# Sparse attention and a squared-ReLU layer in one kernel: the last four blocks' second product as seven half-size products

## The chip, the cores and the metric

The kernel runs on one core of a Trainium2 chip. The metric is device time in microseconds (us) of one execution; the engines are named as in the profile: PE is TensorE (PEld its weight loads), DVE is VectorE, ACT is ScalarE, POOL is GpSimd, SP is SyncE.

## The reference

Two layers follow each other. Attention has 8 batches, 8 heads, 576 positions and 64 columns a head; four heads look back over a local window of 32 positions, four see every 32nd position. The result, as 4608 tokens of 512 columns, goes through two products with a squared ReLU between them.

```python
scores = scale * np.matmul(q, k.transpose(0, 1, 3, 2))
mask_local = (rel >= 0) & (rel < stride)                      # heads 0 to 3
mask_strided = (rel >= 0) & (pos[None, :] % stride == pos[:, None] % stride)   # heads 4 to 7
attn = softmax of the masked scores
x = np.matmul(attn, v), laid out as [4608 tokens, 512]
h = x @ w_in                    # 512 to 2048
r = np.maximum(h, 0.0)
g = s * (r * r) + b
out = g @ w_out                 # 2048 to 512
```

## The kernel before, in words

**Attention.** A batch is four pairs of heads (m = 0, 1 local, m = 2, 3 strided). `pair_steps` writes each pair as steps: transposes of q and k (or transposing DMAs in later batches), scores into a bank of PSUM, exp on ACT and mask on DVE (L529, L537), p times v into an "a" bank (L567), reciprocal and normalisation on DVE (L582, L593) into `x_nat`. x is then transposed into `xT`, [512 columns as 4 × 128, tokens]: by TensorE in early batches (`xtrans`, L615), by a transposing DMA on SP for local pairs from batch 2 (`x_dma`, L645), and for strided pairs from batch 4 by a write to DRAM and a transposing read (`x_out` L637, `x_in` L641). `xT` holds all 4608 tokens.

**The two products.** Tokens are cut into 9 blocks of 512 (T = 0 to 8). The first product (`ff1`, L673) makes for each of the 16 row tiles `ft` four matmuls of 512 columns into one of two "f1" banks; ACT takes the ReLU (`u`, L691), DVE the square (`gT`, L697). `gT` has two buffers, so block T's first product begins after the second product of block T − 2. The second product (`ff2`, L713) takes 128 tokens at a time: 16 matmuls of 512 columns, with a weight load of `gT` before each, into one of two "f2" banks; DVE evicts it with the scale s and the bias row `bcs` (L724), and SP stores it (L728). The factor s and the bias b are folded into this eviction. The last 128 tokens are done as two halves of 256 columns.

**The order.** `Plan` is a small planner that runs while the program is built. Each step has a cost in ns, needs and keys; work of DVE, ACT, GpSimd and the DMA queues is posted with its needs and goes to the engine that ends it first. `Plan.LAT` adds the time until a result is seen: 70 ns for an engine, 12 us for a transposing DMA ("D", "Y"), 7 us for a write to DRAM ("X"). The main loop at the end chooses the next step of TensorE: attention if it is behind its due time (`due`) or nothing else is ready; else the next step of the first product; else of the second. When the first product is more than 64 steps ahead, the second goes first. The hardware then runs each engine's instructions in this order, with waits on what they need.

**PSUM.** Eight banks: t (1), s (2), a (1), f1 (2), f2 (2); `group_of` gives attention its banks.

**Buffers.** In the pool `inp`, the tags qp and kp (paired copies of q and k, later the outputs of transposing DMAs of q) have two buffers each.

Of the kernel before, what the change touches and what calls it, by code (L numbers as in the profile page):

```python
# [9 lines left out]
FP16 = mybir.dt.float16  # L10
# [5 lines left out]
class Plan:  # L16
# [20 lines left out]

    def post(self, needs, cost, fn, keys):
        self.pend.append((needs, cost, fn, keys))

    def flush(self):
        while True:
            best = None
            for p in self.pend:
                r = self.ready_at(p[0])
                if r is not None and r <= self.t and (best is None or r < best[0]):
                    best = (r, p)
            if best is None:
                return
            r, p = best  # L50
            self.pend.remove(p)
            eng = min(p[1], key=lambda e: max(self.free[e], r) + p[1][e])
            end = max(self.free[eng], r) + p[1][eng]
            self.free[eng] = end
            p[2](eng)
            for k in p[3]:
                if isinstance(k, Group):
                    k = ("rel", k.tag, k.n)
                soon = isinstance(k, tuple) and k[0] == "soon"
                self.done[k] = end + (6000.0 if soon else self.LAT[eng])  # L60

# [50 lines left out]
def kernel(  # L112
# [47 lines left out]
    gp = ctx.enter_context(tc.tile_pool(name="gp", bufs=2))  # L160
    op = ctx.enter_context(tc.tile_pool(name="op", bufs=3))
    psum = ctx.enter_context(tc.tile_pool(name="psum", bufs=1, space=bass.MemoryType.PSUM))

    ident = const.tile([128, 128], FP16)
    mask_loc = const.tile([128, LQ], FP16)
    mask_str = const.tile([SQ, SQ], FP16)
    neg_loc = const.tile([128, 2 * LQ], FP16)
    neg_str = const.tile([SQ, 2 * SQ], FP16)
    ones16 = const.tile([128, 128], FP16)
    s_sb = const.tile([128, 1], FP32)  # L170
# [4 lines left out]
    w_out_sb = const.tile([128, NFT, DM], FP16)  # L175
    bcs = const.tile([128, DM], FP32)
    NV = 2
    v_loc = [const.tile([128, 4, LT, D + 1], FP16, name=f"v_loc{i}") for i in range(NV)]
# [4 lines left out]
    qD_str = [const.tile([128, ST, 2, SQ], FP16, name=f"qD_str{i}") for i in range(2)]  # L183
    xT = [const.tile([128, NTOK], FP16, name=f"xT{i}") for i in range(4)]

# [117 lines left out]
    def pair_post(b, name, mm, key):  # L303

        if (b, name) not in paired:
            paired[b, name] = None

        def g(eng):
            if paired[b, name] is None:
                paired[b, name] = inp.tile([128, 2, LT, 2 * D], FP16, tag=name + "p",  # L310
                                           name=name + "p")[0:LQ]
            from_ = loaded[b, name + "l"]
            copy_on(eng, out=paired[b, name][:, mm].rearrange("p j (e d) -> p e j d", e=2),
                    in_=from_.rearrange("p (m e j d) -> p m e j d", m=2, e=2, d=D)[:, mm])
        plan.post([key], {"A": 810, "V": 350, **({"P": 900.0} if b in (1, 2, 3) else {})}, g,
                  [("in", name + "l", b, mm)])
# [34 lines left out]
    def group_of(kind, b, m, q=False):  # L351

        t, a, f1, f2 = ("t", TB), ("a", AB), ("f1", F1B), ("f2", F2B)
        banks = {"a": [a], "t": [t], "s": [("s", SB)]}[kind]
        if b == 0:
            banks = {"a": [f2, f2, f1], "t": [t, a], "s": [("s", SB), ("s", SB), f1]}[kind]
        elif b == 1 and kind == "a":
            banks = [f1, f1, a]
        elif b == 1 and q:
            banks = [t, f2]  # L360
        taken[kind] += 1
        return Group(*banks[taken[kind] % len(banks)])
# [4 lines left out]
    def pair_steps(b, m):  # L367
# [67 lines left out]
        q_by_dma = b >= (QB_DMA if loc else QS_DMA)  # L435
        x_by_dma = b >= (2 if loc else XS_DMA)

# [22 lines left out]
        def q_dma(eng):  # L460
            if loc:
                if (b, "qTl") not in loaded:
                    loaded[b, "qTl"] = inp.tile([128, 2, LT, LQ], FP16, tag="qp", name="qTl")
                st["qT"] = loaded[b, "qTl"][:, mm]
                nc.sync.dma_start_transpose(out=st["qT"],
                                            in_=loaded[b, "ql"][:, 768 * mm:768 * mm + 768])
                return
            if (b, "qT2") not in loaded:
                loaded[b, "qT2"] = inp.tile([128, 2, ST, SR], FP16,
                                            tag="vs" if b < KB_DMA else "kp", name="qT2")  # L470
            st["qT"] = loaded[b, "qT2"][:, mm]
            nc.sync.dma_start_transpose(out=st["qT"],
                                        in_=loaded[b, "qs"][:, 1024 * mm:1024 * mm + 1024])
# [137 lines left out]
        def xtrans(j, group):  # L611
# [10 lines left out]
            if j == nt - 1:  # L622
# [3 lines left out]
                def g(eng):  # L626
                    dst = xT[m][:, b * S:(b + 1) * S]
                    if loc:
                        copy_on(eng, out=dst, in_=st["px"])
                    else:  # L630
                        copy_on(eng, out=dst.rearrange("d (p j) -> d p j", j=nt),
                                in_=st["px"].rearrange("d (j p) -> d p j", j=nt))
                s.posts = [([key], {"A": 640, "V": 455 if loc else 756}, g, [("xT", b, m), group])]
            return s
# [5 lines left out]
        def x_in(eng):  # L640
            nc.sync.dma_start_transpose(out=xT[m][:, b * S:(b + 1) * S],  # L641
                                        in_=x_dram[2 * (b % 2) + mm])

        def x_dma(eng):
            nc.sync.dma_start_transpose(  # L645
                out=xT[m][:, b * S:(b + 1) * S].rearrange("d (t p) -> d t p", t=nt),
                in_=st["x"].rearrange("p t d -> p (t d)"))

        if x_by_dma and loc:
            plan.post([("x", id_, e, nt - 1) for e in range(2)], {"D": 1000.0}, x_dma,  # L650
                      [("xT", b, m)])
        elif x_by_dma:

            plan.post([("x", id_, e, j) for e in range(2) for j in (per - 1, nt - 1)],
                      {"X": 500.0}, x_out, [("xd", id_)])
            plan.post([("xd", id_)], {"Y": 1300.0}, x_in, [("xT", b, m)])
        else:
# [6 lines left out]
    gts = {}  # L664

    def ff1(T, ft, ct, group, cts=(0, 1, 2, 3), early=False):
        tok0 = T * PS
        def f():
            if ft == 0 and ct == cts[0]:
                gts[T] = gp.tile([128, NFT, PS], FP16, tag="gT", name="gT")  # L670
            if ct == cts[0]:
                gts["h", T, ft] = bank(group)
            nc.tensor.matmul(  # L673
                out=gts["h", T, ft], lhsT=w_in_sb[min(ft // 4, 2)][:, ct].rearrange(
                    "p (c x l) -> p c l x", x=128, l=4)[:, max(ft // 4 - 2, 0), ft % 4],
                rhs=xT[ct][:, tok0:tok0 + PS], start=(ct == cts[0]), stop=(ct == cts[-1]))

# [3 lines left out]
        if ft == 0 and ct == cts[0] and T >= 2:  # L681
            needs.append(("F2", T - 2))
        s = Step(f, 216, needs=needs, group=group if ct == cts[0] else None)
        if ct == cts[-1]:
            key = ("h", T, ft)
            s.keys = [key]

# [7 lines left out]
            def sq(eng):  # L695
                u = gts["u", T, ft]
                nc.vector.tensor_tensor(out=gts[T][:, ft, :], in0=u, in1=u, op=ALU.mult)  # L697

            free = [("g", *divmod(NFT * T + ft - 4, NFT))] if T or ft >= 4 else []
            s.posts = [([key] + free, {"A": 600, **({"V": 690} if T == 0 else {})}, rl, [("u", T, ft), group]),  # L700
                       ([("u", T, ft)], {"V": 430}, sq, [("g", T, ft)])]
        return s

    def ff2(T, ts, ft, group, part=0, parts=1):
# [14 lines left out]
        if ft == NFT - 1:  # L719
            s.keys = [id_] + ([("F2", T)] if ts == 3 else [])  # L720

            def ev(eng):
# [5 lines left out]
                nc.sync.dma_start(out=out[r0:r0 + 128, cols], in_=o[:, 0:n])  # L728
            s.posts = [([id_, ("bcs",)], {"V": 750 / parts + 60}, ev, [group])]
        return s  # L730
# [152 lines left out]
    for T in range(NBLK):  # L883
        if T == 0:
# [3 lines left out]
            f1 += [ff1(T, ft, ct, gr[ft], cts, True) for ct in cts for ft in range(4)]  # L888
        for ft in range(0 if T else 4, NFT):
            gr = Group("f2", F2B) if T == 0 and ft % 4 < 2 else Group("f1", F1B)  # L890
            for ct in range(4):
                f1.append(ff1(T, ft, ct, gr))
        if T == 0:

            gr = [Group(*x) for x in [("f2", F2B)] * 4 + [("a", AB)]]
            for c in range(0, NFT, 4):
                f2 += [bcs_step(ft, gr[4]) for ft in range(c, c + 4)]
                f2 += [ff2(T, ts, ft, gr[ts]) for ts in range(2) for ft in range(c, c + 4)]
            f2 += [ff2(T, ts, ft, gr[ts]) for ts in (2, 3) for ft in range(NFT)]
            continue  # L900
        for ts in range(4):

            parts = 2 if T == NBLK - 1 and ts == 3 else 1
            for part in range(parts):
                gr = Group("f2", F2B)
                for ft in range(NFT):
                    f2.append(ff2(T, ts, ft, gr, part, parts))
    def keep_running(until):

# [24 lines left out]
    def due():  # L934

        pos = (i1 + i2) / 64.0 + 0.1
        return (pos if pos <= 1 else 1 + (pos - 1) / 2) * batch_ns

    while i2 < len(f2) or any(at_i[p] < len(att[p]) for p in range(len(att))):
# [15 lines left out]
        if i2 < len(f2):  # L955
            order.append(2)
        if len(order) == 2 and i1 % 4 == 0 and i1 > i2 + 64:
            order.reverse()
# [55 lines left out]
```

## Time and profile before

| | us |
|---|---|
| median of 11 runs (lowest to highest) | 316.79 (315.63 to 318.9) |
| the profiled execution | 315.72 |
| its span, first to last instruction | 314.0 |
| TensorE busy in it | 307.7 |
| VectorE busy | 195.6 |
| ScalarE busy | 160.8 |
| GpSimd busy | 96.2 |

The span is what the trace of one execution covers; the profiled execution's own time is 1.7 us longer. Busy time of TensorE includes the modelled end of each matmul, which overlaps the next one: a mean of 379 ns stands for a matmul, though the next starts 216 ns after it. The distance between starts is what the text uses.

### The profile page before, as it was taken

Reading aid. Unit: us, or ns where it says so; the run is one execution under the profiler, and the core shown is the slowest. Engines: PE = TensorE matmul, PEld = TensorE weight load, DVE = VectorE, ACT = ScalarE, POOL = GpSimd, SP = SyncE. Lnnn points to the kernel's source line nnn. Section 1 sums busy time; section 2 is a strip of 40 time slices with the busy share of each in tenths; the row PEclk is TensorE's granted clock in tenths of the full one; section 3 lists DMA queues with packets and bytes.
Section 4 is the critical chain, followed back from the end, with each engine's and each line's share of the span. In section 5 each row is a group of like instructions: output and inputs, shape, how many; then the busy total and the mean of one; then the engine's idle time right before and its main releaser. Section 6 shows DMA issues by size and latency. Waiting matters only on the chain.

```text
span 314.0 us, 6164 instructions
## 1 busy us (share of the span) xinstructions
PE 307.7 (98%) x2268; PEld 171.2 (55%) x2268; DVE 195.6 (62%) x555; ACT 160.8 (51%) x304; POOL 96.2 (31%) x140
## 2 busy tenths in 40 slices
PE   8899999999999999999999999999999999999995
PEld 3765655666556565556555655555544454444444
DVE  6576868798967797658566867586732254333212
ACT  1876944788838688547037825661531263333100
POOL 7562559902960292058302850000000000000000
PEclk9999999999999999999999999999999999999999
DMA  7999999994999599979997999703041100110022
GB/s 126 201 212 204 215 165 151 221 158 110 79 155 171 85 127 143 147 137 141 163 179 178 123 168 147 185 35 106 21 90 43 57 35 0 67 37 33 34 100 70
DMA packets 99386, 37.84 MB, mean 121 GB/s; under 512 B 82394, under 2 KB 93274, under 8 KB 99354
## 3 DMA queue, kind: packets, MB, share of 16 engines
q0 software_dynamic: 57200, 18.08, 58.0%
q1 hardware_dynamic: 42154, 19.35, 30.5%
q8 instruction: 18, 0.29, 0.4%
q14 instruction: 14, 0.11, 0.1%
HBM read 36.84 MB, written 10.62 MB: 151 GB/s over the span
## 4 chain that ended last, share of the span: by engine, by line
PE 88%; DMA 8%; POOL 1%; issue 0%; SPq 0%; DVE 0%; POOLq 0%
PE ps_f L713 40%; PE ps_f L673 37%; PE ps_s L513 5%; DMA qs<-in_q_dram 4%; PE ps_a L567 4%; DMA w_out_sb<-in_v_dram 2%; DMA ql<-in_q_dram 2%; PE ps_t L395 1%; PE ps_a L736 1%; PE ps_t L615 1%; POOL v_loc L301 1%; PE ps_f L567 0%; SPq L807 0%; PE ps_f L395 0%; POOL ql L259 0%
## 5 line engine op out<-in xcount | busy, mean ns | idle before, releaser
L673 PE MATMUL ps_f<-xT,w_in_sb 128*128 128x512 f16 x568 | 145.5, 379 | 0.0
L713 PE MATMUL ps_f<-w_out_sb,gT 128*128 128x512 f16 (+1 forms) x592 | 144.7, 373 | 0.0
L691 ACT ACTIVATE u<-ps_f 128x512 f16<-128x512 f32 x140 | 82.7, 596 | 97.4 <-PE ps_f L673 84.3
L697 DVE TENSOR_TENSOR gT<-u 128x512 f16<-128x512 f16 x144 | 59.5, 417 | 46.7 <-ACT u L691 45.8
L673 PEld LDWEIGHTS <-w_in_sb 128*128 128x128 f16 x576 | 61.0, 113 | 44.5 <-issue 0.2
L713 PEld LDWEIGHTS <-gT 128*128 128x128 f16 x592 | 55.4, 98 | 52.4 <-DVE gT L697 0.6
L724 DVE SCALAR_TENSOR_TENSOR o<-ps_f,s_sb,bcs 128x512 f32<-128x512 f32 (+1 forms) x37 | 27.0, 729 | 24.9 <-PE ps_f L713 24.5
L593 DVE TENSOR_TENSOR x_nat<-ps_a,rec 72x256 f16<-72x256 f32 (+1 forms) x76 | 35.0, 460 | 1.3
L582 DVE RECIPROCAL rec<-ps_a 72x4 f32<-72x4 f32 (+1 forms) x76 | 13.8, 181 | 22.3 <-PE ps_a L567 21.8
L529 ACT ACTIVATE p_str<-ps_s 72x432 f16<-72x432 f32 (+1 forms) x46 | 20.9, 482 | 4.0 <-PE ps_s L513 3.7
L529 ACT ACTIVATE p_loc<-ps_s 128x384 f16<-128x384 f32 x46 | 21.0, 496 | 3.7 <-PE ps_s L513 3.1
L279 POOL DMA_DIRECT2D v_loc<-in_v_dram x28 | 20.8, 753 | 4.5 <-DMA kl<-in_k_dram 1.3
L567 PEld LDWEIGHTS <-p_str 72*128 72x128 f16 x256 | 15.4, 98 | 11.0 <-issue 0.2
L537 DVE TENSOR_TENSOR p_str<-p_str,mask_str 72x432 f16<-72x432 f16 (+1 forms) x42 | 14.6, 356 | 1.8 <-ACT p_str L529 1.3
L537 DVE TENSOR_TENSOR p_loc<-p_loc,mask_loc 128x384 f16<-128x384 f16 x42 | 14.0, 351 | 2.4 <-ACT p_loc L529 2.0
L768 POOL COPY gate<-kT 1x1 f16<-1x1 f16 x6 | 1.3, 215 | 45.2 <-DMA kT<-ks 45.2
L567 PE MATMUL ps_a<-v_str,p_str 72*128 72x65 f16 x204 | 14.9, 194 | 0.0
L567 PEld LDWEIGHTS <-p_loc 128*128 128x128 f16 x192 | 11.0, 98 | 6.7 <-ACT x_nat L588 0.3
L284 POOL DMA_DIRECT2D v_str<-in_v_dram x16 | 12.9, 814 | 5.1 <-DVE rec L582 2.8
L256 POOL DMA_DIRECT2D kl<-in_k_dram x16 | 11.8, 755 | 0.0
L923 PE MATMUL ps_f<-ones 128*128 128x512 f16 (+2 forms) x30 | 9.3, 446 | 1.4 <-DVE ones L230 1.1
L567 PE MATMUL ps_a<-v_loc,p_loc 128*128 128x65 f16 x150 | 10.5, 194 | 0.0
(116 smaller groups left out, 256.8 us busy)
## 6 DMA issues: line engine op xcount, KB each, us to landing
out_dram<-o SPq DMA_DIRECT2D x35, 256.0 KB, 4.4
w_out_sb<-in_moe_w_out_dram POOLq DMA_DIRECT2D x4, 512.0 KB, 11.1
v_loc<-in_v_dram POOLq DMA_DIRECT2D x28, 72.0 KB, 7.6
ql<-in_q_dram POOLq DMA_DIRECT2D x6, 288.0 KB, 7.0
qs<-in_q_dram POOLq DMA_DIRECT2D x6, 288.0 KB, 5.9
ks<-in_k_dram POOLq DMA_DIRECT2D x6, 288.0 KB, 7.2
kl<-in_k_dram POOLq DMA_DIRECT2D x4, 288.0 KB, 8.6
kl<-in_k_dram POOLq DMA_DIRECT2D x16, 72.0 KB, 4.2
```

The costliest lines, as they stand in the source:

```text
L279: nc.gpsimd.dma_start(out=vl[LPAD:128, h, :, 0:D], in_=v_band(b, h))
L513: nc.tensor.matmul(out=st["s", g][0:nk, c:c + 2 * nq], lhsT=(st["k"][:, i * nq:i * nq + nk] if loc else st["k"][:, i, 0:SQ]), rhs=st["q"][ ...
L529: nc.scalar.activation(out=pt[0:nk, 0:2 * n].rearrange("k t c -> k (t c)"), in_=st["s", g][0:nk, 0:2 * n * nq], func=AF.Exp, scale=scale)
L537: nc.vector.tensor_tensor(out=pt[0:nk, 0:2 * n], in0=pt[0:nk, 0:2 * n], in1=mask, op=ALU.mult)
L567: nc.tensor.matmul(out=st["a"][:, j % per, :], lhsT=st["pw", g][0:nk, i * nq:i * nq + WIDE], rhs=vt[0:nk, 2 * mm + e, j, :])
L582: nc.vector.reciprocal(out=st["rec", e, j][0:nq, 0:per], in_=st["pa", e, j][0:nq, 0:per, D:D + 1])
L593: nc.vector.tensor_tensor(out=st["x"][:, j0:j0 + per, 64 * e:64 * e + 64], in0=st["pa", e, j][0:nq, 0:per, 0:D], in1=st["rec", e, j][0:nq, ...
L673: nc.tensor.matmul(out=gts["h", T, ft], lhsT=w_in_sb[min(ft // 4, 2)][:, ct].rearrange("p (c x l) -> p c l x", x=128, l=4)[:, max(ft // 4 ...
L691: nc.scalar.activation(out=gts["u", T, ft], in_=gts["h", T, ft], func=AF.Relu)
L697: nc.vector.tensor_tensor(out=gts[T][:, ft, :], in0=u, in1=u, op=ALU.mult)
L713: nc.tensor.matmul(out=gts[id_], lhsT=gts[T][:, ft, ts * 128:(ts + 1) * 128], rhs=w_out_sb[:, ft, cols], start=(ft == 0), stop=(ft == NFT ...
L724: nc.vector.scalar_tensor_tensor(out=o[:, 0:n], in0=gts[id_], scalar=s_sb[:, 0:1], in1=bcs[:, cols], op0=ALU.mult, op1=ALU.add)
```

## The change

For blocks 5 to 8 (`SEVEN = 5`) the second product is computed in the form that makes a product of 2 × 2 blocks from seven block products (`ff2_seven`). The four blocks of the left side are halves of a block's 512 tokens by halves of the 2048 rows; those of the right side halves of those rows by halves of the 512 output columns. A product P1 to P7 is 2 × 8 matmuls of 256 columns. It needs:

- four differences of weights, once, after the second product of block 4 (`mix_post`): three into new tiles `w_mix`, one in place in `w_out_sb`; and the difference of the two halves of `bcs`;
- four sums of blocks of `gT` per block, each in two parts (`sums_post`), on DVE. In blocks 5 and 6 two of them overwrite `gT` itself once P1 and P2 have read it; in blocks 7 and 8 (`roomy`) they have tiles of their own;
- evictions that add what earlier evictions left: Va, Ua, Vb, and Ub = Ua + the difference of the bias on DVE or GpSimd; four stores of [128, 2, 256] per block (five in block 8). P2 continues the bank of P1 after Va is out, P4 that of P7 after Vb, P3 that of P5 after its store's eviction.

The order of products is P1 P2 P6 P7 P5 P4 P3 in blocks 5 and 6, all in the two f2 banks, and P1 P6 P7 P5 P2 P4 P3 in blocks 7 and 8, in four banks (f2 and s, then t, a and f1). The first product of blocks 5 to 8 takes its row tiles in the order 0-3, 8-11, 4-7, 12-15, and its squares may go to ACT too.

With it come: `xT` as a ring of four batches, whose writes wait for the first product that read the slot (`x_free`), and whose edge splits block 4's first-product matmuls in two; three shared buffers "pp" for what qp, kp and the later qT2 had; the small masks and `ones16` as views of `w_mix`; banks a and t in turn for p times v from batch 4 on; and the strided pairs of the last batch transposed by TensorE, the local pairs of the last batch with 4 us in the plan for their transposing DMA. The place of a step in its block (`pos`) replaces the count of steps in `due` and in the rule of the lead.

```diff
+    NX = 4
+    xT = [const.tile([128, NX * S], FP16, name=f"xT{i}") for i in range(4)]
+    def x_free(b):
+        return [("F1", (S * (b - NX + 1) - 1) // PS)] if b >= NX else []
...
+        elif b >= KB_DMA and kind == "a":
+            banks = [a, t]
...
-        x_by_dma = b >= (2 if loc else XS_DMA)
+        x_by_dma = b >= 2 if loc else XS_DMA <= b < B - 1
...
+    def sums_post(T):
+        at2, at4 = ("S2", "S4") if roomy(T) else ((0, 0), (0, 1))
+        for h in range(2):
...
+            plan.post(gl + free, ns, make("S", (0, 0), (1, 0), ALU.subtract), [("S", T, 3, h)])
+            plan.post(gh + [("S", T, 3, h)], ns, make((1, 0), (1, 0), (1, 1), ALU.add),
+                      [("S", T, 1, h)])
+            plan.post([("S", T, 1, h), ("P1", T - 1 if roomy(T) else T)], ns,
+                      make(at2, (1, 0), (0, 0), ALU.subtract), [("S", T, 2, h)])
+            plan.post([("S", T, 2, h), ("P6", T - 1) if roomy(T) else ("P2", T)], ns,
+                      make(at4, (0, 1), at2, ALU.subtract), [("S", T, 4, h)])
+    def mix_post():
+        jobs = ((3, wr[1], wr[0]), (1, wr[0], wl[0]), (2, wr[1], w_mix[1]), (4, wl[1], w_mix[2]))
+        before = [("F2", SEVEN - 1)]
+        for i, x, y in jobs:
+            plan.post(before, {"V": 1250.0}, ...
+                          out=w_mix[i], in0=x, in1=y, op=ALU.subtract), [("w_mix", i)])
+            before = [("w_mix", i)]
...
+    def ff2_seven(T):
+        banks = {NBLK - 1: (("t", TB), ("a", AB), ("f1", F1B), ("f1", F1B)),
+                 NBLK - 2: (("f2", F2B), ("f2", F2B), ("s", SB), ("s", SB))}
+        X, W, Y, Z = [Group(*x) for x in banks.get(T, [("f2", F2B)] * 4)]
...
+        seq = [
+            ("P1", X, "X", True, cut(0, 0), w(0, 0), gn(0), [],
+             [([d("P1"), ("bcs",)], EV, ev("Va", "X", lambda: b1), [d("Va")])]),
+            ("P5", W, "W", True, cut(1, 0), mix(1), sn(1), wait(1), []),
+            ("P2", X, "X", False, cut(0, 1), w(1, 0), gn(1), [d("Va")],
+             [([d("P2")], EV, store(0, 0, "X", lambda: b1), [X])]),
+            ("P6", Y, "Y", True, tile_of("S2") if roomy(T) else cut(0, 0), mix(2), sn(2), wait(2),
+             [([d("P6"), d("Va")], EV, ev("Ua", "Y", val("Va")), [d("Ua"), Y]),
+              ([d("Ua"), ("dbc",)], add_ns, add_db, [d("Ub")])]),
+            ("P7", Z, "Z", True, tile_of("S"), mix(3),
+             sn(3), wait(3),
+             [([d("P7"), d("Ub")], EV, ev("Vb", "Z", val("Ub")), [d("Vb")]),
+              ([d("P5"), d("Vb")], EV, store(1, 1, "W", val("Vb")), [d("C22")])]),
+            ("P4", Z, "Z", False, cut(1, 1), mix(4), gn(1), [d("Vb")] + wait(4),
+             [([d("P4")], EV, store(1, 0, "Z", val("Ua")), [Z])]),
+            ("P3", W, "W", False, tile_of("S4") if roomy(T) else cut(0, 1), w(1, 1), sn(4), [d("C22")],
+             [([d("P3")], EV, store(0, 1, "W", val("Ub")), [W])]),
+        ]
+        seq = [seq[i] for i in ((0, 3, 4, 1, 2, 5, 6) if roomy(T) else (0, 2, 3, 4, 1, 5, 6))]
+        for key, group, name, fresh, lhs, rhs, needs, more, posts in seq:
+            for t in range(2):
+                for k in range(H):
...
+                        nc.tensor.matmul(out=gts[name, T][:, t], lhsT=lhs(k, t), rhs=rhs(k),
...
+            at = tok0 % (NX * S)
+            n = min(PS, NX * S - at)
+            for lo, hi in ((0, n), (n, PS))[:1 + (n < PS)]:
+                nc.tensor.matmul(
+                    out=gts["h", T, ft][:, lo:hi],
...
+                       ([("u", T, ft)], {"V": 430, **({"A": 600} if T >= SEVEN else {})}, sq, [("g", T, ft)])]
...
-        pos = (i1 + i2) / 64.0 + 0.1
+        pos = i1 / 64.0 + (f2[i2 - 1].pos if i2 else 0.0) + 0.1
...
-        if len(order) == 2 and i1 % 4 == 0 and i1 > i2 + 64:
+        if len(order) == 2 and i1 % 4 == 0 and i1 / 64.0 > (f2[i2 - 1].pos if i2 else 0.0) + 1:
```

## The prediction

> **What bounds the kernel now.** I read the busy table and the slices of the page first, then the chain that ended last, then a table by stage, then the end of the timeline.
>
> ```profile
> PE 307.7 (98%) x2268; PEld 171.2 (55%) x2268; DVE 195.6 (62%) x555; ACT 160.8 (51%) x304; POOL 96.2 (31%) x140
> PE   8899999999999999999999999999999999999995
> DVE  6576868798967797658566867586732254333212
> PEclk9999999999999999999999999999999999999999
> PE 88%; DMA 8%; POOL 1%; issue 0%; SPq 0%; DVE 0%; POOLq 0%
> ```
>
> TensorE is busy in every slice but the first two and the last, at full clock, and the chain is TensorE for 88%; the rest of it is the loads at the head. Since busy is not the same as at its peak, I checked the pace: in the chain, runs such as 5 matmuls in 1.08 us and 12 in 2.59 us give 216 ns for a 512-column matmul all through. So from about 40 us on, TensorE issues at its limit, and only a shorter TensorE stream (or a hole in it) moves the end.
>
> The stages after the fifth block, in the table by stage (columns: length; then busy us of TensorE, weight loads, VectorE, ScalarE, GpSimd; clock, DMA share, GB/s):
>
> ```profile
> 195.20:211.40 16.20, 16.20 (x106) 9.04 (x105) 11.95 (x35) 10.51 (x21) 0.00 (x0) 1.00 0.44 111
> 211.40:236.97 25.57, 25.57 (x157) 13.24 (x156) 13.86 (x38) 8.96 (x15) 0.00 (x0) 1.00 0.29 67
> 236.97:247.80 10.83, 10.83 (x52) 4.95 (x51) 2.59 (x4) 0.60 (x1) 0.00 (x0) 1.00 0.19 73
> 269.10:292.20 23.10, 23.10 (x108) 11.48 (x107) 8.45 (x18) 8.96 (x15) 0.00 (x0) 1.00 0.10 35
> 292.20:310.60 18.40, 18.36 (x101) 9.70 (x99) 4.58 (x8) 0.60 (x1) 0.00 (x0) 1.00 0.21 79
> ```
>
> By counting matmuls in the timeline, the second product of block 4 ends at 211.4 us, those of blocks 5 and 6 begin at 211.4 and 240.4; blocks 7 and 8 follow at 268 and 295.7. VectorE is 74% busy just before 211.4, 54% in the next stretch, and 24 to 38% later; GpSimd has no work after 195 us. That is the room that the change spends.
>
> The price of a half-size matmul is already in this profile, because the last 128 rows are done as two halves:
>
> ```profile
> 303.65 0.75 DVE L724 SCALAR_TENSOR_TENSOR o<-ps_f,s_sb,bcs 128x512 f32<-128x512 f32 x1 [2.70 <-PE ps_f L713]
> 307.11 0.75 DVE L724 SCALAR_TENSOR_TENSOR o<-ps_f,s_sb,bcs 128x512 f32<-128x512 f32 x1 [2.70 <-PE ps_f L713]
> 308.85 0.48 DVE L724 SCALAR_TENSOR_TENSOR o<-ps_f,s_sb,bcs 128x256 f32<-128x256 f32 x1 [0.99 <-PE ps_f L713]
> 310.60 0.48 DVE L724 SCALAR_TENSOR_TENSOR o<-ps_f,s_sb,bcs 128x256 f32<-128x256 f32 x1 [1.26 <-PE ps_f L713]
> ```
>
> Evictions start as their sixteen matmuls end: 307.11 − 303.65 = 3.46 us for 512 columns (216 ns each), 310.60 − 308.85 = 1.75 us for 256 (109.4 ns each), each with its own weight load (98 ns), which stays hidden.
>
> [...]
>
> **The change, part by part.**
>
> *Seven products.* A block goes from 64 matmuls of 512 columns to 7 × 16 = 112 of 256: 64 × 215.8 = 13.81 us to 112 × 109.3 = 12.24 us, −1.57. Block 8 had 48 × 215.8 + 32 × 109.3 = 13.86 us, −1.62. Sum 3 × 1.57 + 1.62 = **−6.33 us**, all on TensorE, which sets the end.
>
> *xT as a ring of 4 × 576 columns.* Only block 4 (tokens 2048 to 2559 over the edge at 2304) is split: its 64 first-product matmuls become 128 halves, 128 × 109.3 − 64 × 215.8 = **+0.18 us**. The new wait is that batch b's xT waits for the first product of block b−3 or so. For batch 7 that is block 4: it ends near 177 us, and the first write of batch 7 is the transposing DMA of 213.6 us, 36 us later. What is queued behind it on SP, the stores of outputs, sees nothing. Zero, covered by how far attention trails the ring.
>
> *Last outputs transposed by TensorE.* For the two strided pairs of batch 7, 2 writes to DRAM (0.49 us of SP each) and 2 transposing reads (2.07 and 1.17 us of SP) go; 16 transposes come, at 33 ns (4 in 0.13 us in the timeline near 105 us): **+0.52 us** of TensorE; and two copies, 0.64 us on ScalarE or 0.76 on VectorE. The last read was issued at 232.5 us and its kind lands in 6.4: block 7 could start from about 239 and starts at 247.8, the 10.8 us before it filled by 50 second-product matmuls. In the new order block 7 can start about 10 us sooner. No time by itself, since no hole was there, but its first product then covers the waits of block 6's seven products.
>
> *Two banks for p·v from batch 4 on.* In 217 to 226 us the pairs of four p·v matmuls stand 1.2 us apart, filled with other work. I price it at nothing; it gives the order more to put into holes near 211 us.
>
> *Shared input buffers (three for four).* By the order of use, the long wait would be the queries' transposing DMA at 152.3 us, which takes the buffer last read by the spreads of batch 4, at 115.4. Nothing waits.
>
> *VectorE.* Per block: [...] seven evictions for four, + 3 × 0.74 = 2.2; [...] Four blocks: about 31 us; once, four weight differences of 2048 elements, 4 × 1.22 = 4.9, and 0.4 for the bias. 36 us over the 100 us from 211 to the end, where VectorE now works about 37. The squares may go to ScalarE (0.6 us each), which is idle for half of that time. Whether Square needs a table load is not shown (the one load of the trace costs 1.28 us); bounds 0 and some 10 loads on an engine with slack; I take 0.
>
> *The new waits.* A product that continues a bank waits for its eviction: about 0.2 us until the matmul's result is seen, 0.74 for the eviction, 0.1 to release: **1.05 us**, four times a block (the second after the first in X; the others have one or two products, 1.75 to 3.5 us, between them). In blocks 7 and 8 four separate banks and an order with at least one product between make all covered. In blocks 5 and 6 the first product of the next block, 13.8 us of TensorE, is the cover. Bounds: below, 0 (all covered; a gain is excluded, because TensorE has no holes to fill); above, 16 × 1.05 = 16.8 us. At block 5 comes a wait for the third weight difference: 3.7 us of VectorE at 54% load is about 8 us, so 219.4 us. TensorE has until then 3.5 us of products 1 and 2, 56 p·v matmuls (1.85 us), and block 6's first product, whose last input lands near 208. I take one uncovered eviction at block 5 and a little for the rest: **+1.2 us**.
>
> *The end.* After the last first product, 28 half-size matmuls of block 7 and 112 of block 8, 15.3 us against 17.3. The last eviction is again 256 columns with one DMA behind it: the 3.4 us after 310.6 stay.
>
> **Sum.** −6.33 + 0.18 + 0.52 + 1.2 = −4.4 us. The profiled execution took 315.72 us (span 314.0 and 1.7 around it), 1.07 below the median of 316.79. So 311.3 for such an execution, **312.4 us** against the median, 1.4% faster. Within 0.5% (1.6 us, 315.2 to 318.4) is about what a measurement of this kernel can tell from no change.
>
> **Rivals.**
>
> *All waits covered* (chance 0.12): −6.33 + 0.70 = −5.6, so 311.2. For it: the room on VectorE after 236 us. Against: the crowding at 211 us.
>
> *VectorE becomes the bound around block 5* (0.16). Between 211.4 and 237 it works 13.9 us of 25.6; added are 5.3 once, 5.5 of sums (half of block 5's, half of block 6's), 2.2 of evictions and 0.7: 27.6, over by 2 us even before any queueing; attention's normalisations and the releases of first-product banks stand in the same queue. If TensorE sees twice that, 4 us, the time is 315.2 (range 314 to 317). Against: 16 squares (6.7 us) may move to ScalarE.
>
> *The evictions are not covered* (0.10, slower). If first-product steps are not there when a product waits, because they wait themselves for the buffer that the same late second product holds, each block pays. From 5.6 / 4 = 1.4 us a block, that is more than one uncovered eviction, nothing is left; at two, 8.4 us, the time is 316.8 − 5.6 + 8.4 = 319.6. For it: block T+2's first product needs the second product of block T done. Against: the order begins block T only when a quarter of block T+1 is emitted.
>
> *Half-size matmuls do not run at 109 ns.* With weight loads exposed a block would take 112 × 207 ns; 32 of them in a row exclude it above. No chance given.
>
> **From cases to numbers.** The forecast has 0.62 (311 to 314). Faster: 0.62 + 0.12 + 0.06 of the VectorE case = 0.80; same: the other 0.10 of it; slower 0.10. The range leaves out the slower case and the top of the VectorE case: 310.2 to 316.5.
>
> **What would show it.** TensorE again busy 98 to 99% with some 300 matmuls more; 448 matmuls of 256 columns at 109 ns; no TensorE idle over 1 us after 40 us except at 211 to 220; VectorE near 232 us in all. I am wrong if the list of waits shows TensorE waiting for VectorE for more than 4 us together, if the half-size matmuls stand further apart, or if block 7 still starts after block 6 has run out of cover.

## The result, and the profile after

The changed kernel takes 312.86 us (median of 12 runs; 311.46 to 314.64) against 316.75 us for the kernel before (47 runs, the 11 of the table further up among them). The ratio is 0.988, 95% interval 0.986 to 0.990: 3.8 us, or 1.2%, faster. The forecast was 312.4 us. The profiled execution took 311.46 us.

The page of the changed kernel, first the busy times, then three rows of the slices:

```profile
PE 302.3 (98%) x2524; PEld 195.6 (63%) x2524; DVE 215.4 (70%) x573; ACT 182.3 (59%) x341; POOL 96.7 (31%) x140
PE   8999999999999999999999999999999999999993
DVE  6576858898967888747664875579776467747552
PEclk9999999999999999999999999999999999999999
```

TensorE is still busy to the end, with 256 matmuls more: 448 where the last four blocks had 272, 64 more where block 4 is split, 16 transposes. VectorE and ScalarE took up 20 and 21.5 us. The stages that answer to those of before are cut at the first matmul of block 5's second product (212.3 us), where the first products of block 7 (240.6) and block 8 (266.7) begin, just behind the start of the second products of blocks 6 and 7, and at the end of the last first product (288.9):

```profile
195.20:212.30 17.10, 17.10 (x120) 9.60 (x119) 13.30 (x39) 11.16 (x22) 0.00 (x0) 1.00 0.68 135
212.30:240.60 28.30, 28.08 (x228) 19.86 (x227) 20.55 (x42) 17.02 (x30) 0.00 (x0) 1.00 0.11 35
240.60:266.70 26.10, 26.10 (x179) 18.20 (x177) 16.83 (x30) 13.08 (x22) 0.00 (x0) 1.00 0.11 40
266.70:288.90 22.20, 22.20 (x144) 14.72 (x142) 11.92 (x21) 12.78 (x22) 0.00 (x0) 1.00 0.11 37
288.90:305.60 16.70, 16.12 (x147) 14.07 (x144) 9.82 (x14) 1.19 (x2) 0.00 (x0) 1.00 0.27 95
```

VectorE is at 73% around block 5 and 65% around block 6: crowded, but not full. TensorE loses 0.22 us around block 5 and 0.58 in block 8, nothing else. The list of waits, from the last matmul of the bias row at 49.6 us on, for TensorE, is two lines long:

```profile
PE ps_a L833 <- DVE o L771: 0.6, 1, 0.6
PE ps_f L862 <- ACT u L884: 0.2, 1, 0.2
```

The first one is at the very end. In the timeline of the last microseconds it can be seen whole:

```profile
302.97 1.26 PE L833 MATMUL ps_a<-w_out_sb,S 128*128 128x256 f16 x10
...
304.26 0.48 DVE L771 SCALAR_TENSOR_TENSOR o<-ps_a,s_sb,Ub 128x256 f32<-128x256 f32 x1 [0.34 <-PE ps_a L833]
304.80 0.82 PE L833 MATMUL ps_a<-w_out_sb,S 128*128 128x256 f16 x6 [0.57 <-DVE o L771]
...
305.65 0.48 DVE L771 SCALAR_TENSOR_TENSOR o<-ps_a,s_sb,Ub 128x256 f32<-128x256 f32 x1 [0.91 <-PE ps_a L833]
```

Block 8's last product P3 is evicted in two halves, so that its first half leaves early. Both halves lie in one bank. Eight matmuls of the first half and two of the second are issued; then VectorE reads the first half, and the last six matmuls stand until it has. Ten matmuls at 0.109 us would have let the eleventh start at 304.06; it starts at 304.80, so 0.74 us are lost.

**A mark that makes single profiles comparable.** The profiles differ at the head: TensorE is busy 35.4 to 37.5 us of the first 40, as the first loads land. The changed kernel was profiled twice. The start of the last matmul of the bias row, which is the mark, lay at 49.6 us in one profile and 50.5 in the other, and from there to TensorE's last end both took 256.0 us. The kernel before, profiled once, took 260.5 us. This length is used below beside the ratios, whose intervals are 0.3 to 0.6% wide. That it repeats rests on these two profiles.

| kernel | to TensorE's last end, us | ratio to before (95% interval) |
|---|---|---|
| before | 260.5 | |
| changed | 256.0 | 0.988 (0.986 to 0.990) |
| changed, again | 256.0 | 0.985 (0.983 to 0.988) |
| no seven products | 261.2 | 1.004 (1.003 to 1.005) |
| last x through DRAM | 257.2 | 0.987 (0.984 to 0.990) |
| one bank for p·v | 256.3 | 0.988 (0.985 to 0.991) |
| last product not split | 255.2 | 0.984 (0.981 to 0.987) |
| last product in two banks | 255.2 | 0.983 (0.981 to 0.986) |
| seven products from block 4 | 254.9 | 0.982 (0.979 to 0.984) |
| block 8 in the order of 5 and 6 | 257.0 | 0.989 (0.986 to 0.992) |
| squares on VectorE | 256.0 | 0.985 (0.983 to 0.988) |
| from block 4, and two banks | 254.9 | 0.984 (0.982 to 0.986) |
| from block 3, and two banks | 271.9 | 1.035 (1.031 to 1.038) |

### The profile page after: what moved, and what is told of

It is laid out like the page before. It is cut to its first block, busy times and chain, and to the rows that moved or that the text cites. A ratio compares the mean times of both kernels' runs of the same rounds, so it can differ in the third digit from the quotient of the medians.

```text
span 309.7 us, 6706 instructions
## 1 busy us (share of the span) xinstructions
PE 302.3 (98%) x2524; PEld 195.6 (63%) x2524; DVE 215.4 (70%) x573; ACT 182.3 (59%) x341; POOL 96.7 (31%) x140
## 4 chain that ended last, share of the span: by engine, by line
PE 92%; DMA 3%; ACT 2%; POOL 1%; DVE 1%; issue 0%; ACTq 0%; POOLq 0%
PE ps_f L862 39%; PE ps_f L911 22%; PE ps_f L833 12%; PE ps_s L528 5%; DMA vs<-in_v_dram 3%; PE ps_a L582 3%; PE ps_s L833 2%; PE ps_t L408 2%; PE ps_a L833 1%; PE ps_t L582 1%; PE ps_a L934 1%; PE ps_t L833 1%; PE ps_t L630 1%; PE ps_f L582 1%; PE ps_s L862 0%; ACT p_str L544 0%
## 5 line engine op out<-in xcount | busy, mean ns | idle before, releaser
L862 PE MATMUL ps_f<-xT,w_in_sb 128*128 128x512 f16 (+1 forms) x632 | 146.6, 357 | 0.2 <-ACT u L884 0.2
L862 PEld LDWEIGHTS <-w_in_sb 128*128 128x128 f16 x640 | 68.0, 113 | 35.7 <-issue 0.8
L911 PE MATMUL ps_f<-w_out_sb,gT 128*128 128x512 f16 x320 | 85.0, 379 | 0.0
L893 DVE TENSOR_TENSOR gT<-u 128x512 f16<-128x512 f16 x112 | 46.3, 418 | 32.9 <-ACT u L884 32.2
L911 PEld LDWEIGHTS <-gT 128*128 128x128 f16 x320 | 29.2, 98 | 23.6 <-DVE gT L893 0.6
L833 PEld LDWEIGHTS <-gT 128*128 128x128 f16 x320 | 31.1, 98 | 8.4
L833 PE MATMUL ps_f<-w_out_sb,gT 128*128 128x256 f16 x176 | 24.5, 273 | 0.0
L608 DVE TENSOR_TENSOR x_nat<-ps_a,rec 72x256 f16<-72x256 f32 (+1 forms) x52 | 23.8, 457 | 0.5
L891 ACT ACTIVATE gT<-u 128x512 f16<-128x512 f16 x32 | 19.8, 629 | 0.8
L922 DVE SCALAR_TENSOR_TENSOR o<-ps_f,s_sb,bcs 128x512 f32<-128x512 f32 x20 | 14.9, 746 | 5.2 <-PE ps_f L911 4.9
L833 PEld LDWEIGHTS <-S 128*128 128x128 f16 x128 | 12.4, 98 | 4.0 <-issue 0.8
## 6 DMA issues: line engine op xcount, KB each, us to landing
out_dram<-o SPq DMA_DIRECT2D x35, 256.0 KB, 4.6
```

What stands on the lines that cost most here:

```text
L608: nc.vector.tensor_tensor(out=st["x"][:, j0:j0 + per, 64 * e:64 * e + 64], in0=st["pa", e, j][0:nq, 0:per, 0:D], in1=st["rec", e, j][0:nq, ...
L833: nc.tensor.matmul(out=gts[name, T][:, t], lhsT=lhs(k, t), rhs=rhs(k), start=fresh and t == k == 0, stop=t == 1 and k == H - 1, skip_group ...
L862: nc.tensor.matmul(out=gts["h", T, ft][:, lo:hi], lhsT=w_in_sb[min(ft // 4, 2)][:, ct].rearrange("p (c x l) -> p c l x", x=128, l=4)[:, ma ...
L891: nc.scalar.activation(out=gts[T][:, ft, :], in_=u, func=AF.Square)
L911: nc.tensor.matmul(out=gts[id_], lhsT=gts[T][:, ft, ts * 128:(ts + 1) * 128], rhs=w_out_sb[:, ft, cols], start=(ft == 0), stop=(ft == NFT ...
```

## The experiments

**Everything but the seven products.**

```diff
-    SEVEN = 5
+    SEVEN = 9
...
-            mix_post()
+            if SEVEN < NBLK:
+                mix_post()
```

> Everything of the change but the seven products: all nine blocks take their second product as 64 matmuls of 512 columns; the ring of xT, the shared buffers, the two p-times-v banks and the TensorE transposes of the last batch stay. My theory (the time is TensorE's issue): +0.18 us for block 4's split and +0.52 us for 16 transposes against the kernel before, so a ratio of 1.002 and a span near 314.7 us, VectorE busy within 2 us of before. Rival (the other parts fill holes and bring part of the gain themselves): a ratio of 0.997 or less.

TensorE's end comes 0.7 us later than before (261.2 for 260.5), which is the sum of the two terms. VectorE has 192.0 us, 3.6 less than before, where I had allowed 2. The ratio gives 1.2 us (interval 0.8 to 1.7), some 0.5 us more than TensorE's stream shows; in the profile, TensorE's last end is followed by 4.0 us here and by 3.4 before (why is told at the end of this section). So the other parts of the change, taken together, bring no time by themselves; the seven products bring 5.2 us net (261.2 to 256.0), and the other parts are its price and its cover.

**The last batch's strided outputs through DRAM again.** The local pairs get their old 12 us in the plan too.

```diff
-        x_by_dma = b >= 2 if loc else XS_DMA <= b < B - 1
+        x_by_dma = b >= (2 if loc else XS_DMA)
...
-                      [("xT", b, m)], 4000.0 if b == B - 1 else None)
+                      [("xT", b, m)])
```

> The changed kernel, but the last batch's strided outputs go through DRAM and a transposing read again and the local pairs have their old 12 us in the plan. My theory: 0.52 us of TensorE come off, but block 7's first product can start only some 10 us later, so products of block 6 stand without cover and wait for evictions, 1.05 us each: two to four of them, +1.6 to +3.7 us net against the changed kernel (ratio to before 0.993 to 1.0). Rival (cover isn't needed, because the seven products hardly wait): -0.5 us, ratio 0.9865.

The timeline of TensorE in this kernel:

```profile
239.12 3.66 PE L833 MATMUL ps_f<-w_out_sb,gT 128*128 128x256 f16 x32
244.38 1.91 PE L833 MATMUL ps_f<-w_out_sb,gT 128*128 128x256 f16 x16 [1.61 <-DVE Va L760]
246.12 1.91 PE L833 MATMUL ps_f<-w_mix,gT 128*128 128x256 f16 x16
247.90 1.91 PE L833 MATMUL ps_f<-w_mix,S 128*128 128x256 f16 x16
...
250.19 1.89 PE L862 MATMUL ps_f<-xT,w_in_sb 128*128 128x512 f16 x8
```

Without first-product steps (none until 250.19), block 6 goes P3 of block 5, P1, then P2, which waits for Va. One wait, not two to four; but a longer one: it would have started at 239.12 + 32 × 0.1093 = 242.62, so 1.76 us are lost. VectorE's timeline says why:

```profile
242.37 1.29 DVE L714 TENSOR_TENSOR gT<-gT 128x1024 f16<-128x1024 f16 x2 [0.56 <-PE ps_f L833]
243.59 0.74 DVE L760 SCALAR_TENSOR_TENSOR Va<-ps_f,s_sb,bcs 128x512 f32<-128x512 f32 x1
```

The two halves of the sum that overwrites a part of `gT` wait for the same P1 and stand ahead of Va in VectorE's queue: 1.3 us. So TensorE's end comes 1.2 us later than in the changed kernel (1.76 − 0.52), which is below the range I gave. The rival falls by the trace; by the ratio alone the two kernels can't be told apart. Behind TensorE's last end this kernel takes 3.4 us where the changed one takes 4.1 (see the end of this section), so its span ends only some 0.5 us later.

**One bank for p·v.**

```diff
-        elif b >= KB_DMA and kind == "a":
-            banks = [a, t]
```

> The changed kernel, but p times v has the one bank a again from batch 4 on. My theory: I priced the second bank at nothing; the time stays within 0.5 us of the changed kernel (ratio 0.987 to 0.990), with the last p-times-v matmuls later than in the changed kernel. Rival (the bank is what fills TensorE around the start of block 5's seven products): TensorE stands still for 1 us or more between 205 and 230 us and the ratio is 0.992 or more.

One wait of 0.52 us appears at 217.4 us, for Va in block 5, the 0.22 us of the changed kernel are gone, and TensorE's end comes 0.3 us later. The last p-times-v matmuls are later, as expected (230.5 for 226.7 us). TensorE's end puts the second bank at 0.3 us; the ratio can't tell it from nothing.

**The last product not split.**

```diff
-                    if k == H - 1 and key == "P3" and last:
+                    if False:
```

> The changed kernel, but block 8's last product is evicted and stored once, [128, 2, 256], not in two halves. In the changed kernel the second half's last 6 matmuls waited 0.57 us for VectorE to read the first half from the same bank. My theory (that wait and what follows it is a good part of the 1.3 us by which the gain fell short): the wait is gone, the end has one eviction of 0.75 us for 0.48, net -0.3 us, ratio about 0.987; no TensorE wait after 300 us. Rival (the split hides the store, and the wait only moved the end by nothing): +0.3 to +0.5 us, because the last store is 256 KB for 128.

The wait is gone and TensorE ends 0.7 us sooner, as the 0.74 us from the timeline would have it; the last eviction is 0.75 us for 0.48. So the last store starts 0.5 us sooner. But it has 256 KB for 128, and SyncE, which waits for it at the end of the program, goes on 2.27 us after the last eviction's end, for 1.77 us in the changed kernel. From the mark that is 258.30 us for 258.26: for the landing of the last store the split brings nothing and costs nothing. The rival was right that the split helps the store (0.5 us); my theory was right about the wait. The end of the span still comes 0.4 us sooner here, through what SyncE does after the store (see the end of this section). The ratio of 0.984 has an interval that overlaps the changed kernel's two (0.988 and 0.985), so a gain from leaving the split out isn't shown.

**The last product's halves in two banks.** P5 and P3 of block 8 take the second half of their rows from a bank s.

```diff
-                        nc.tensor.matmul(out=gts[name, T][:, t], lhsT=lhs(k, t), rhs=rhs(k),
+                        nc.tensor.matmul(out=gts["W2" if two and t else name, T][:, t],
+                                         lhsT=lhs(k, t), rhs=rhs(k),
...
-                                    [W] if t else [("C12", T)])]
+                                    [W2] if t else [W, ("C12", T)])]
```

> The changed kernel, but in block 8 the two row halves of products P5 and P3 lie in two banks (a and s), so the last half can be added while VectorE reads the half before it; the halves are evicted separately. From the last matmul of the bias row (near 50 us) to TensorE's last end the changed kernel has 256.0 us, the kernel before 260.5. My theory: as without the split, 255.1 us, and the last eviction is 0.48 us, not 0.75: 0.3 us less than without the split, ratio about 0.983 to 0.985. Rival (the end is set by the store, not by the bank): no difference to the changed kernel, 0.988.

TensorE now runs on while VectorE reads the half before, but the last eviction found a new wait:

```profile
304.51 1.04 PE L839 MATMUL ps_s<-w_out_sb,S 128*128 128x256 f16 x8
304.72 0.48 DVE L774 SCALAR_TENSOR_TENSOR o<-ps_a,s_sb,Ub 128x256 f32<-128x256 f32 x1
305.89 0.48 DVE L774 SCALAR_TENSOR_TENSOR o<-ps_s,s_sb,Ub 128x256 f32<-128x256 f32 x1 [0.69 <-DMA out_dram<-o]
```

There are three output tiles, and the fourth eviction from the end has to have left for HBM first. That takes back what the shorter eviction gives: the last eviction ends as it does without the split (256.1 for 256.0 us from the mark). Its store is the smaller one, and SyncE goes on behind it at 257.8 us from the mark, 0.4 us sooner than in the changed kernel.

**Seven products from block 4.**

```diff
-    SEVEN = 5
+    SEVEN = 4
```

> The changed kernel with seven products from block 4 on: one block more, whose sums, evictions and weight differences fall into the time in which VectorE still normalises attention. Theory that TensorE's issue sets the time: 1.57 us less, 254.4 us from the last bias matmul to TensorE's last end, ratio 0.983. Rival (VectorE becomes the bound there): waits of TensorE for VectorE of 1.6 us or more between 160 and 215 us take the gain back, ratio 0.988 or above.

TensorE ends 1.1 us sooner than in the changed kernel: 1.57 less one new wait of 0.7 us, for a normalisation of attention at 215 us, and without the changed kernel's wait of 0.22 us. VectorE works 25.3 of the 30 us from 185 to 215 here, 21.1 in the changed kernel. Part of each theory: TensorE's issue sets the time, and VectorE begins to show.

**Block 8 in the order of blocks 5 and 6.**

```diff
-        seq = [seq[i] for i in ((0, 3, 4, 1, 2, 5, 6) if roomy(T) else (0, 2, 3, 4, 1, 5, 6))]
+        seq = [seq[i] for i in ((0, 3, 4, 1, 2, 5, 6) if roomy(T) and not last else (0, 2, 3, 4, 1, 5, 6))]
```

> The changed kernel, but block 8 takes its products in the order of blocks 5 and 6 (P2 straight behind P1 in one bank), where no first product is left to stand between. This prices one uncovered eviction. My theory: P2 waits for Va, 1.05 us (0.2 until the product is seen, 0.75 eviction, 0.1), and nothing else: 257.0 us from the last bias matmul to TensorE's last end. Rival (one late eviction delays the whole chain behind it): 2 us or more.

```profile
292.51 1.91 PE L833 MATMUL ps_t<-w_out_sb,gT 128*128 128x256 f16 x16
295.26 1.91 PE L833 MATMUL ps_t<-w_out_sb,gT 128*128 128x256 f16 x16 [0.84 <-DVE Va L760]
297.00 3.66 PE L833 MATMUL ps_f<-w_mix,S 128*128 128x256 f16 x32
```

P2 could start at 292.51 + 16 × 0.1093 = 294.26 and starts at 295.26: 1.0 us for one uncovered eviction, where I had put 1.05. Nothing behind it is late; TensorE ends 1.0 us later.

**All squares on VectorE.**

```diff
-                       ([("u", T, ft)], {"V": 430, **({"A": 600} if T >= SEVEN else {})}, sq, [("g", T, ft)])]
+                       ([("u", T, ft)], {"V": 430}, sq, [("g", T, ft)])]
```

> The changed kernel, but all squares of blocks 5 to 8 stay on VectorE (32 went to ScalarE, 19.8 us of it). VectorE gets 32 x 0.418 = 13.4 us, 229 us in all. My theory: TensorE has first-product steps to go on with, so the time moves by less than 0.5 us (256.0 to 256.5 us from the last bias matmul to TensorE's last end). Rival of the prediction (VectorE is the bound around block 5): waits of TensorE for VectorE or ScalarE of 2 us and more between 205 and 245 us, 258 us or more.

256.0 us, not a tenth more, with VectorE at 224.2 us, 8.8 more than in the changed kernel. VectorE isn't the bound around block 5, even with 32 squares more.

**The parts put together, from block 4 and from block 3.** Both have the two banks at the end, by the edit shown above, and evict the very last half into Vb's buffer. The second run has `SEVEN = 3`.

```diff
-    SEVEN = 5
+    SEVEN = 4
...
-                o = op.tile([128, 2, 256], FP32, tag="o", name="o")
+                o = (cp.tile([128, 2, 256], FP32, tag="V", name="oV") if last and ts.start else
+                     op.tile([128, 2, 256], FP32, tag="o", name="o"))
```

> Seven products from block 4 on, block 8's P5 and P3 in two banks each, and the very last half evicted into the free buffer of Vb, since with two banks it waited 0.69 us for the store three before it to land. If the parts add up: seven products from block 4 gave 254.9 us from the last bias matmul to TensorE's last end, two banks took 0.75 us off the changed kernel's 256.0: 254.1 us, and the last eviction starts as its half ends, so 4.8 us less than the kernel before at TensorE's end and more at the store: ratio 0.979 to 0.981. If the end is set by the stores' landing instead, no better than seven products from block 4 alone, 0.9815.

The wait for the store is gone, but the gains don't add up: 254.9 us, where 254.1 was expected. Two waits for normalisations near 215 us, 0.39 and 0.74 us by the timeline, stand where seven products from block 4 alone had one, of 0.7. The changed kernel has 0.985 on the same chip, so the ratio shows no gain over it, and TensorE's end is where seven products from block 4 alone put it. That simpler version, 0.982, has the lowest ratio of all, though its interval overlaps those of several others.

> The same with seven products from block 3 on. If TensorE's issue still sets the time: 1.57 us less than from block 4, 252.6 us, ratio 0.975. If VectorE is the bound by then (it works 27 of 40 us between 120 and 160 us and 29 of 40 to 200 us already, and 8 us a block come in): TensorE waits for VectorE by 1.6 us or more between 130 and 215 us, ratio 0.981 or more.

This is slower than the kernel before, and not as expected: 271.9 us to TensorE's last end, 19.3 more than the theory of TensorE's issue gives. The line from TensorE's timeline:

```profile
190.27 0.52 PE L528 MATMUL ps_s<-qD_str,kT 128*72 128x144 f16 x3 [13.97 <-POOL qD_str L312]
```

and what GpSimd did until then:

```profile
171.34 0.18 POOL L975 COPY gate<-kT 1x1 f16<-1x1 f16 x1 [16.68 <-DMA kT<-ks]
...
185.72 0.80 POOL L295 DMA_DIRECT2D v_str<-in_v_dram  x1 [1.22 <-DMA qs<-in_q_dram]
188.03 0.80 POOL L295 DMA_DIRECT2D v_str<-in_v_dram  x1 [1.51 <-DMA ks<-in_k_dram]
188.83 1.39 POOL L312 COPY qD_str<-qT 64x576 f16<-64x576 f16 x2
```

The plan gave a spread of q to GpSimd, since VectorE and ScalarE were taken (in the changed kernel GpSimd has only loads, and small copies that wait for them, in these 50 us). But GpSimd's queue also issues the loads, which wait for buffers; the spread of 1.39 us came behind them, and TensorE behind the spread. That VectorE's load drove it there is argued from the planner's rule; the 14 us behind GpSimd's queue are shown.

The wait is not all of the loss. The page of this run has TensorE's busy share and the clock that it was granted (both in tenths, in 40 slices of 8.2 us):

```profile
PE   8889999999999999999995077999999999999995
PEclk9999999999999999999999567999999999999999
```

Behind the wait TensorE goes on at half its clock until about 194 us: the first 10 half-size matmuls, from 190.59 us, take 2.13 us, 213 ns each, where it was 109 ns. A second wait, 1.57 us for Va at 201.2 us, is followed by half clock again, until about 204.4 us. The mean granted clock was 0.83 from 160 to 200 us and 0.96 from 200 to 240; the changed kernel has 1.00 in both. The two waits are 15.5 us, and half of the some 7 us at half clock is 3.5: together about 19 of the 19.3 us. A wait of this size for VectorE is what the rival had expected; it is the smaller part.

**The changed kernel once more**, on the chip of these two.

> The changed kernel once more, on the chip of the two combinations, for a comparison on one chip and a second profile. 256.0 us from the last bias matmul to TensorE's last end if everything behind the head repeats; the time from there to the end of the span 3.4 or 4.1 us if the final store's landing varies from execution to execution, 4.1 again if the change lengthened it. Ratio 0.986 to 0.990.

256.0 us again. From TensorE's last end to the end of the span there are 4.1 us, as the first time; 3.4 in the profile of the kernel before. From the end of the last eviction to the end of the span it is 2.9 us in the kernel before and with the last x through DRAM, and 3.5 to 3.6 in all other profiles, the one without seven products included. So the seven products don't cause it.

Nor does the store itself. At the end of the program SyncE carries out nine waits for semaphores, one after the other, and the trace has each of them. The wait that belongs to the last store is over 1.75 to 1.77 us after the last eviction in all twelve profiles with a last store of 128 KB. In the kernel before and with the last x through DRAM this wait is the sixth, three stand behind it, and the span ends 1.11 us later. In the other ten it is the second, seven stand behind it, and the span ends 1.75 to 1.81 us later. (Without the split it is the last, and the span ends 1.34 us later.) So the 0.7 us is work of SyncE that runs while the store is on its way in one order and after it in the other. Both kernels with the short end send the last batch's strided x through DRAM; why the place in the order changes with it is not shown.

## Why the prediction was right, by its steps

- **Half-size matmuls at 109 ns**: right. In block 8 of the changed kernel, P6 and P7 together are 32 matmuls in 297.73 − 294.23 = 3.50 us, 109.4 ns each. The term of −6.33 us stands: 5.2 us net between the kernel without seven products and the changed one, with 0.22 + 0.74 us of waits in between and 0.2 unaccounted for. The pace is the one of the kernel before, 216 ns at 512 columns (12 matmuls in 2.59 us) and 109.4 ns at 256 (16 in 1.75 us), there too with a weight load for each.
- **The split of block 4 and the transposes, +0.70**: right, 0.7 measured.
- **The stall of 1.2 us**: its sum was near (0.96 us) by luck, its place wrong. I put one uncovered eviction at the start of block 5. There was none: P1 and P2 of block 5 were drawn out over 212 to 227 us between first-product steps, and the third weight difference, for which I allowed until 219.4, was ready at 218, while P6 began at 227. The loss was in block 8, in the split of P3's eviction, which I had called the same end as before. I had looked for a wait in products that continue a bank, not in two halves of one product in the same bank. The price that I had for such a wait, an estimate, holds there too: 0.2 and 0.1 us around an eviction of 0.48 make 0.78. In the timeline above it is 0.20 us from the end of the ten matmuls (304.06) to the eviction's start, 0.48 for the eviction and 0.06 to the next matmul (304.74 to 304.80), 0.74 together; with two banks the wait is gone.
- **3.4 us behind TensorE's last end**: mis-sized, 4.1, through the waits of SyncE that stand behind the last store. With it the predicted −4.4 us is −4.5 at TensorE's end and −3.8 in the runs. I had looked at the store and not at what the program does after it.
- **VectorE near 232 us**: 215.4. Part of it is that 32 squares went to ScalarE; with all of them on VectorE it is 224.2, still 8 less. The parts other than the seven products take off 3.6 of these (192.0 us for 195.6 without seven products), and one addition went to GpSimd there (0.7); the rest isn't explained. The 36 us that I had added were my estimate; of its parts only the eviction (0.74) was shown by the profile before. Measured in the changed kernel: 0.68 us for each of the eight sums of a block (5.5 together, as allowed), 0.69 for an addition, 1.19 to 1.21 for each of the four weight differences (4.8 for 4.9) and 0.41 for the bias. The one addition that GpSimd took, with the squares kept on VectorE, measured 1.27 us. For the squares on ScalarE (629 ns each) no table load came in: the trace has one load, of 1.28 us, as before.
- **Block 7 about 10 us sooner**: 7.2 (240.6 for 247.8), because it then waits for the second product of block 5 to free `gT`. That it serves as cover is shown by the run through DRAM.
- **Rivals**: VectorE as the bound around block 5 fell (squares on VectorE: no change). The uncovered eviction costs what was said, 1.0 us, and 1.8 with two halves of a sum ahead of it; it simply occurs nowhere in the changed kernel but at the end. For the seven products themselves the rival of all waits covered was nearer than my forecast: but for the split of the last eviction they cost TensorE one wait of 0.22 us, and without the split TensorE ends 5.2 us sooner than before, where that rival had 5.6.

## What to carry to other kernels

When one engine is at its issue limit (here TensorE, a matmul every 216 or 109 ns), price a change by that engine's instructions and then ask of every new wait what stands ahead of it in its engine's queue: an eviction behind two halves of a sum cost 1.8 us where a bare one cost 1.0. Before the last eviction is split, look whether the halves lie in different banks and whether an output tile is free: here the split cost 0.74 us in one bank, which its smaller store gave back, and in two banks the last half waited 0.69 us for a tile. Work that the planner moved to an idle-looking engine came behind that engine's DMA issues and their waits: here 14 us for a copy of 1.4. And a wait can cost more than its length: behind the 14 us TensorE worked at half its clock for almost 4 (213 ns for a half-size matmul that took 109).

## What the runs showed that I had not expected

From a mark behind the head, the length of the program repeated to a tenth of a microsecond (256.0 and 256.0 us), while whole executions spread over 3 us; between the two profiles the difference lies in the first loads. The end of the program has a part that the busy times don't show: the place of the last store's wait among the nine closing waits of SyncE moved the end by 0.7 us.
